# A planned TensorE order whose planner also counts the arrival of instructions, with its priorities set anew

## The chip, the core and the metric

The kernel runs on one core of a Trainium2 chip. The time is device microseconds (us) of one execution, the median over runs. The core's engines are PE (TensorE; PEld is its weight loads), DVE (VectorE), ACT (ScalarE), POOL (GpSimd) and SP (SyncE, which here only issues DMAs). Each engine executes its own instructions strictly in the order of the program; between engines there are semaphores.

## The reference

Three stages follow each other. Stage 1 is a delta-rule recurrence over 768 positions, for 2 batches of 8 heads of width 48; stage 2 a dense block over the 1536 tokens that it yields; stage 3 a mixture of 8 experts, one expert for each token.

```python
for t in range(S):                                   # stage 1
    y[:, :, t] = np.einsum('bhd,bhde->bhe', q[:, :, t], state)
    v_old = np.einsum('bhde,bhd->bhe', state, kt)    # kt: normalised k
    state = state + bt[..., None] * np.einsum('bhd,bhe->bhde', kt, vt - v_old)
h = x @ w_in                                         # stage 2: 1536x384 @ 384x1024
solu = h * softmax(h)
x = layernorm(solu) * g_ln @ w_out                   # back to 1536x384
logits = x @ w_gate; expert_idx = argmax(logits)     # stage 3
y = relu(x[of expert e] @ w1[e]) @ w2[e]             # scattered back, times the gate
```

## The kernel before, in words

**Stage 1** cuts the 768 positions into 24 chunks of 32, in 3 groups of 8 chunks (numbered 0 to 2). A group is first solved, without the recurrence: products of its keys and queries (`gram`, L522, tile G), a triangular solve on DVE (`prep`: transposition L593, 28 small steps L602 and L605, transpositions L613 and L615), and then the joins of its halves (`join`, L635 and L650, tile Z). Then `stream` walks through its chunks, one after the other, because each needs the state of the one before: the state times keys and queries (L717, tile X), DVE's subtraction (L722, R), the solved triangle times it (L730), scaling on ACT (L738) and DVE (L696), the state's increment (L745, dS), DVE's addition (L690, S), and the chunk's output (L759). The first L717 of chunk 8 thus waits for the solve of group 1, that of chunk 16 for the solve of group 2.

**Stage 2** goes by rows of 128 tokens, 12 of them; four chunks give two rows. A row's function `rows` transposes it (L884, xp), multiplies by w_in (L912, 18 matmuls of 512 columns, tile h), takes maximum, exponential and product on DVE and ACT (L922, L926, L930), transposes back (L951, lp), and multiplies by w_out (L961, 24 matmuls, tile xb). The weights come as 64-bit words and are converted once, in 6 blocks of w_in and 8 of w_out: a load (L785), four DVE operations (L793, L795, L798, L801), a split in two halves on ACT and POOL (L808, L810), and for w_out a small product with the gate weights on PE (L840, tp; L850, gp).

**Stage 3**, from the first L1398 on, has an order written out by hand, which the change does not touch.

**What sets the order.** Stages 1 and 2 are written as coroutines (chains: `rows`, `stream`, `prep`, `wi_block` and so on). When the program is built, the class `Flow` runs them through a list scheduler: each chain asks for an engine with an expected duration, and of the chains that could start, the one with the lowest priority number goes next (`_pick`). The priorities stand in the table `PR` (L54). `Flow.use` books a TensorE step; where TensorE would have nothing to do, `run` puts filler matmuls (L1250) there. The order in which the chains are served becomes the order of the instructions on PE, DVE, ACT and POOL, and of the DMAs on SP; nothing of it is decided at run time.

On SP a DMA waits only where its data or buffer does. `loads_1` (`PR['l1']`) loads group 1's inputs, and starts with a tiny gate DMA (L402, `kn<-A`) that reads a result of group 0, so that everything behind it in SP's order starts only then. `f32_block` (L785; `PR['wi']`) loads a block of w_in; its chain also waits for the planner's event `early`, but the DMA itself has no such wait: it is held back only by what stands ahead of it on SP.

An instruction of the source is not always one on the chip. An fp32 matmul of stage 1 is executed as two, each with its own weight load: "x16" in the program's order is 32 matmuls in the trace, and 64 instructions.

Of the kernel before, what the change touches and what calls it, by code (L numbers as in the profile page):

```python
# [25 lines left out]
DM = H * D  # L26
# [4 lines left out]
E = 8  # L31
# [19 lines left out]
EVA = (0, 1, 1)  # L51
HB = 0
HC = C // 2
PR = {'m0': 4.99, 'x0': 4.63, 'g1': 4.24, 'g2': 3.44, 'lg': 6.61, 'l1': 1.43, 'l2': 3.47, 'wi': 2.29, 'wo': 5.01, 'wog': 1.18, 'n1': 1.36, 'n2': 4.17, 'p1': 4.79, 'p2': 8.87, 'v': 8.16, 'y': 5.65, 'rows': 2.82, 'sx': 3.04, 'xt': 6.94, 'lt': 3.58, 'ft': 2.8}  # L54
PASSES = ((0, 0), (0, 1), (1, 0))
PE, DVE, ACT, POOL, DMA = range(5)
DENSE = 0
# [51 lines left out]
class Flow:  # L109
# [2 lines left out]

    TICK, COLS, FILL = 3.4133, 2800, (0.215, 0.43, 512, 32)
    LAT = {PE: 0.2, DVE: 0.13, ACT: 0.15, POOL: 0.08, DMA: 2.0}

    def __init__(self, pace, cap, until):
        self.req = {e: [] for e in self.LAT}
        self.free = {e: 0.0 for e in self.LAT}  # L120
        self.pending = deque()
        self.cur = None
        self.rate, self.cap, self.fill = pace * self.COLS / self.TICK, cap, None
        self.level = self.at = 0.0
        self.floor, self.until = 1500, until
        self.cols = {}
        self.banks, self.fill_bank = {}, "h"
        self.mode, self.pool = DENSE, 0.0
        self.n = self.live = 0
# [107 lines left out]

    def use(self, t, us):
        cold = not self.warm(t)
        mode = us[3] if len(us) > 3 else DENSE  # L240
        us, cols = us[cold] + (0.0 if mode == self.mode else 0.22 if cold else 0.115), us[2]
        self.mode = mode
        i, f = divmod((t + us) / self.TICK, 1)
        f = min(1, f * self.TICK / us)
        self.cols[int(i)] = self.cols.get(int(i), 0) + cols * f
        self.cols[int(i) - 1] = self.cols.get(int(i) - 1, 0) + cols * (1 - f)
        self.level = min(self.cap, max(-self.floor, self.level - self.rate * (t + us - self.at)) + cols)
        self.at = self.free[PE] = t + us
        return us


def _mm(n):

    return 0.448e-3 * n + 0.003, n / 1200 + 0.002, n

KQ, BLK, DS, GRAM2, GRAM1, WG = (0.96, 1.65, 520, 1), (0.37, 0.62, 152, 2), (0.67, 1.14, 634, 1), \  # L260
    (0.52, 0.88, 520, 3), (0.44, 0.72, 320, 3), (0.7, 1.4, 50)


def _dv(n):
# [16 lines left out]
def build(tc, I, out, cap, dbg=None, pace=1.15, room=100):  # L281
# [7 lines left out]
    pactx = ExitStack()  # L289
    fl = Flow(pace, room, PR['ft'] * 10)  # L290

    with ctx:
# [261 lines left out]
        def grams(g, cs, kss):  # L554
            for ks in kss:
                for c in cs:
                    yield from gram(g, c, ks)
                    fl.loose()
# [8 lines left out]
        def prep(g):  # L567
# [11 lines left out]
            AM[g] = (A, M, mw)  # L579
            fl.spawn(grams(g, range(0, GC, 2), ((0, 1),)), (prio, PR['g1'], PR['g2'])[g])  # L580
            if g:
# [81 lines left out]
        xt = {}  # L663
# [9 lines left out]
        def y_copy(c):  # L673
            s, j = divmod(c, 4)
            for r in range(4):
                if r:
                    fl.loose()
                yield ACT, _ac(192), False, f"X{c % 2}"
                p = 32 * (r ^ 1)
                nc.scalar.copy(out=xt[s][32 * j:32 * j + 32, :, 96 * r:96 * r + 96]  # L680
                               .rearrange("p b (l d) -> p b l d", l=2),
                               in_=ps_[c % 2][p:p + 32, :, r % 2].rearrange("p (b l) d -> p b l d", b=2))
            event("s1", c).set()
            if j == 3:
                for b in range(B):
                    tile_x(b, s)
# [13 lines left out]
        def stream():  # L700
# [3 lines left out]
            for c in range(NC):  # L704
# [51 lines left out]
                for q in range(4):  # L756
                    for r in range(4):
                        p, t = 32 * r, 32 * (r ^ 1)
                        nc.tensor.matmul(ps[t:t + 32, q, r % 2], lhsT=M[p:p + 32, cc * 4 + q],  # L759
                                         rhs=ub[p:p + 32, q, r % 2], start=False, stop=True, skip_group_check=True)  # L760
                fl.spawn(y_copy(c), PR['y'])
                if c < NC - 1:
# [4 lines left out]
        wi = [s2w.tile([128, KT, F], F32R, name=f"wi{k}") for k in range(2)]  # L767
        wo = [s2w.tile([128, FT, DM + E], F32R, name=f"wo{k}") for k in range(2)]
# [51 lines left out]
        def wo_block(t):  # L820
# [12 lines left out]
        def wo_gate(t, wf):  # L833

            yield WT_
            yield T_
            yield PE, (KT * 0.109, KT * 0.2, KT * 250)
            tp = psT.tile([128, KT, 128], F32, name="tp", tag="t")
            for k in range(KT):
                nc.tensor.transpose(tp[:, k], wf[:, 128 * k:128 * k + 128], idn)  # L840
            event("wT", t).set()
            yield ACT, _ac(DM)
            wT = wd.tile([128, KT, 128], F32, name="wT")
            nc.scalar.copy(out=wT, in_=tp)
            T_.release()
            yield T_
            yield PE, WG
            gp = psT.tile([128, E], F32, name="gp", tag="t")
            for k in range(KT):
                nc.tensor.matmul(gp, lhsT=wT[:, k], rhs=wg[:, k], start=(k == 0), stop=(k == KT - 1))  # L850
            WT_.release()
            yield DVE, _dv(E)
            nc.vector.tensor_copy(out=wo[0][:, t, DM:], in_=gp)
            yield DVE, _dv(E)
            nc.vector.tensor_tensor(out=wo[1][:, t, DM:], in0=gp, in1=wo[0][:, t, DM:].bitcast(F32), op=ALU.subtract)
            T_.release()
            event("wog", t).set()


        xbx = psH.tile([128, 512], F32, name="xb")  # L860
        nc.vector.memset(xbx[0:32, DM + E:], 0.0)
        xb = xbx[:, :DM + E]
# [6 lines left out]
        def tile_x(b, s):  # L869
            fl.spawn(rows(b, s), PR['rows'] + 0.01 * count[0])  # L870
            count[0] += 1

        def rows(b, s):
            j = b * TPB + s
            x = xt[s][:, b]
            if dbg and "x" in dbg:
                nc.sync.dma_start(out=dbg["x"][128 * j:128 * j + 128], in_=x)
            prio, fl.cur.prio = fl.cur.prio, PR['xt'] + 0.01 * j
            yield XT_
# [18 lines left out]
            h = h_.popleft()  # L898
            event("h", j).set()
            if fl.fill_bank == "h":  # L900
                fl.fill_bank, fl.FILL, spare[0] = "xb", (0.056, 0.11, 120, 32), xbx[0:32, DM + E:]
            fl.cur.prio = prio
            for n in range(2):
                for i, (a, w) in enumerate(PASSES):
# [14 lines left out]
            lg = s2.tile([128, 4, E], F32, name="lg", bufs=4)  # L919
# [50 lines left out]
            lt, m8, i8, le = (lg[:, k] for k in range(4))  # L970
# [275 lines left out]
        spare = [h_[0][0:32, :512]]  # L1246
# [136 lines left out]
        for e in range(E):  # L1383
            n = CAPS[e]
# [184 lines left out]
```

## Time and profile before

| | before |
|---|---|
| median of 3 runs | 478.85 us (477.11 to 483.55) |
| profiled execution | 477.91 us, of which its span 476.1 us |
| stages 1 and 2 (to the first L1398 matmul) | 325.0 us of the span |
| PE busy | 425.9 us (89%) |
| DVE busy | 291.8 us (61%) |
| filler matmuls (L1250) | 145 |

The span runs from the first to the last instruction. Busy shares say little by themselves: what a stage waits for is seen in its stretch. In a timeline, "[2.55 <-issue]" ahead of an instruction is idle time of the engine in which it waited for nothing that the profile shows. A row "x32" is 32 instructions, and successive PE groups overlap by a few hundredths of a microsecond. A row of the windows has the stretch, its length, each engine's busy time with the number of instructions, then PE's granted clock as a share, the DMA engines' busy share and GB/s.

### The profile page before, as it was taken

The page shows a single profiled execution, that of the slowest core. Times are in us where ns is not written, and L with a number is a line of the kernel's source. Part 1 is how long each engine was busy: PE and PEld are TensorE (multiplying, and loading weights), DVE is VectorE, ACT ScalarE, POOL GpSimd, SP SyncE. Part 2 cuts the span into 40 slices and gives each one's busy share as a digit, 9 for nine tenths or more (in the row PEclk, how much of TensorE's full clock was granted, in tenths as well). Part 3 has the DMA queues.
Part 4 walks back from the last instruction along what each step waited for, and adds up shares of the span by engine and source line. Part 5 has one row for each costly group of instructions (what it writes and reads, how often), then busy time and mean ns, then how long its engine had stood idle before and what let it go on. Part 6 is the DMA issues. An engine that isn't in the chain of part 4 may idle for free.

```text
span 476.1 us, 16248 instructions
## 1 busy us (share of the span) xinstructions
PE 425.9 (89%) x6941; PEld 374.2 (79%) x6941; DVE 291.8 (61%) x839; ACT 240.8 (51%) x556; POOL 168.8 (35%) x177
## 2 busy tenths in 40 slices
PE   2328978989999999999999999999999999999983
PEld 2228765767787887867677899898999999999982
DVE  5698998885222668845365587655566555456630
ACT  3023574866223644626354676544665666567520
POOL 1303753112031130021022233323685469658811
PEclk9999995988659999999999999999999999999998
DMA  8265342241000402202111311305984567568000
GB/s 313 84 252 183 134 158 71 66 159 65 4 3 6 168 3 87 100 12 96 69 37 36 134 35 44 140 35 167 361 267 140 189 222 251 190 215 274 17 25 29
DMA packets 17076, 57.57 MB, mean 121 GB/s; under 512 B 2456, under 2 KB 8454, under 8 KB 16226
## 3 DMA queue, kind: packets, MB, share of 16 engines
q1 hardware_dynamic: 15170, 51.70, 31.4%
q0 software_dynamic: 1824, 4.73, 2.7%
q8 instruction: 56, 0.92, 0.8%
q14 instruction: 26, 0.21, 0.1%
HBM read 45.96 MB, written 11.13 MB: 120 GB/s over the span
## 4 chain that ended last, share of the span: by engine, by line
PE 72%; DVE 13%; issue 5%; ACT 4%; DMA 3%; POOL 1%; SPq 0%; POOLq 0%; DVEq 0%; ACTq 0%
PE h L912 12%; PE u L1398 12%; PE xb L961 11%; PE o L1343 10%; PE X L717 5%; PE dS L745 3%; PE G L522 3%; PE lp L951 2%; PE X L759 2%; PE o L1436 2%; DMA out<-y,ti 2%; PE Z L650 2%; PE X L730 1%; DMA kqT<-kqT 1%; DVE wu L798 1%
## 5 line engine op out<-in xcount | busy, mean ns | idle before, releaser
L1215 POOL TENSOR_TENSOR wh<-wr,wh 128x512 fp32r<-128x512 f32 x64 | 81.3, 1301 | 22.7 <-ACT wh L1213 18.6
L912 PE MATMUL h<-wi,xT 128*128 128x512 f32 x216 | 66.6, 434 | 0.0
L961 PE MATMUL xb<-wo,lT 128*128 128x392 f32 x288 | 63.5, 360 | 0.0
L1343 PE MATMUL o<-wh,hT 128*128 128x384 f32 (+1 forms) x336 | 63.1, 340 | 0.0
L1398 PE MATMUL u<-xdT,wh 128*128 128x240 f32 (+1 forms) x504 | 60.4, 278 | 2.2 <-DVE hT L1402 2.2
L1398 PEld LDWEIGHTS u<-xdT,wh 128*128 128x128 f32 x504 | 59.0, 189 | 2.8 <-DVE hT L1402 2.6
L1343 PEld LDWEIGHTS o<-wh,hT 128*128 128x128 f32 (+1 forms) x336 | 57.5, 182 | 0.2
L961 PEld LDWEIGHTS xb<-wo,lT 128*128 128x128 f32 x288 | 50.1, 191 | 2.3
L912 PEld LDWEIGHTS h<-wi,xT 128*128 128x128 f32 x216 | 39.6, 199 | 8.2
L1213 ACT CAST wh<-wr 128x512 fp32r<-128x512 f32 x67 | 41.0, 616 | 3.4 <-DMA wr<-w 3.4
L680 ACT COPY xt<-X 32x192 f32<-32x192 f32 x96 | 29.7, 310 | 25.7 <-PE X L759 24.4
L1402 DVE SCALAR_TENSOR_TENSOR hT<-u,hT 128x240 fp32r<-128x240 f32 (+2 forms) x64 | 24.8, 408 | 26.4 <-ACT hT L1401 26.3
L1401 ACT ACTIVATE hT<-u 128x240 fp32r<-128x240 f32 (+2 forms) x64 | 23.9, 376 | 24.0 <-PE u L1398 21.3
L717 PEld LDWEIGHTS X<-S,kqT 48*64 48x64 f32 x768 | 28.2, 153 | 5.2 <-issue 3.8
L522 PE MATMUL G<-kqT 48*32 48x64 f32 x768 | 19.8, 269 | 13.1 <-DMA kqT<-kqT 8.5
L717 PE MATMUL X<-S,kqT 48*64 48x48 f32 x768 | 31.3, 238 | 0.0
L1355 POOL DMA_INDIRECT out<-y,ti x17 | 16.5, 971 | 38.9 <-DMA out<-y,ti 11.4
L522 PEld LDWEIGHTS G<-kqT 48*32 48x32 f32 x768 | 16.5, 140 | 15.6 <-DMA kqT<-kqT 8.5
L1121 POOL DMA_INDIRECT xs<-xo,posi x12 | 12.5, 1043 | 41.1 <-ACT lT L990 13.6
L738 ACT ACTIVATE ub<-X,slot 128x96 f32<-128x96 f32 x48 | 13.7, 337 | 26.1 <-PE X L730 25.1
L1209 DVE CAST wh<-wp 128x512 fp32r<-128x512 f32 x29 | 20.0, 691 | 9.8 <-ACT wp L1208 8.5
L745 PE MATMUL dS<-ub,kn 64*48 64x96 f32 x368 | 23.8, 279 | 2.2 <-ACT ub L738 2.2
(197 smaller groups left out, 763.9 us busy)
## 6 DMA issues: line engine op xcount, KB each, us to landing
wr<-w SPq DMA_DIRECT2D x32, 768.0 KB, 5.4
kqT<-kqT SPq DMA_DIRECT2D x6, 1024.0 KB, 9.0
xs<-z SPq DMA_DIRECT2D x5, 772.0 KB, 3.9
w<-w_in SPq DMA_DIRECT2D x6, 512.0 KB, 4.9
w<-w_out SPq DMA_DIRECT2D x8, 384.0 KB, 3.1
kn<-kN SPq DMA_DIRECT2D x3, 768.0 KB
vt<-vN SPq DMA_DIRECT2D x3, 768.0 KB, 6.9
xd<-xs SPq DMA_DIRECT2D x10, 193.0 KB, 4.7
```

What stands on the lines that cost most here:

```text
L522: nc.tensor.matmul(G[32 * r:32 * r + 32, c2 * 4 + Q], lhsT=kq[:, r1], rhs=x, start=True, stop=True)
L680: nc.scalar.copy(out=xt[s][32 * j:32 * j + 32, :, 96 * r:96 * r + 96] .rearrange("p b (l d) -> p b l d", l=2), in_=ps_[c % 2][p:p + 32, :, ...
L717: nc.tensor.matmul(ps[64 * o:64 * o + 64, q, r1], lhsT=T[p, c % HG, q // 2, r1, q % 2], rhs=S_[p, q, r1], start=(q == 0 and r1 == 0), stop ...
L745: nc.tensor.matmul(dS[64 * o:64 * o + D, q], lhsT=kn_t[g][64 * o:64 * o + 64, cc, q], rhs=ub[64 * o:64 * o + 64, q], start=False, stop=Tru ...
L912: nc.tensor.matmul(h[:, FH * n:FH * n + FH], lhsT=xT[a][:, k], rhs=wi[w][:, k, FH * n:FH * n + FH], start=(m == 0), stop=(m == 3 * KT - 1))
L961: nc.tensor.matmul(x2, lhsT=lT[t // 4][a][:, t % 4], rhs=wo[w][:, t], start=(t == 0 and i == 0), stop=(t == FT - 1 and i == 2))
L1213: nc.scalar.copy(out=hl[0][:, cs], in_=r[:, cs])
L1215: (nc.vector if k == 1 else nc.gpsimd).tensor_tensor(out=hl[1][:, cs], in0=r[:, cs], in1=hl[0][:, cs].bitcast(F32), op=ALU.subtract)
L1343: nc.tensor.matmul(o, lhsT=hT[t][a][:, s:s + n], rhs=w[k][:, t % 4], start=(t == 0 and i == 0), stop=(t == FT - 1 and i == 2))
L1398: nc.tensor.matmul(u, lhsT=w[c][:, k, f0:f0 + 128], rhs=xT[a][:, k], start=(i == 0 and k == 0), stop=(i == 2 and k == KT - 1))
L1401: nc.scalar.activation(out=hh[0], in_=u, func=AF.Relu)
L1402: nc.vector.scalar_tensor_tensor(out=hh[1], in0=u, scalar=0.0, in1=hh[0].bitcast(F32), op0=ALU.max, op1=ALU.subtract)
```

## The change

The planner's TensorE step gets a count of instructions. After each 256 of them, the next step cannot end before the preceding 256 were begun plus `FETCH` = 3.0 us. Each kind of step says how many instructions it has (64 for a join's half, 64 for L717, 32 for L745, 2 for a plain matmul). And 18 of the 21 priorities are different numbers. No instruction is added or taken out besides fillers: 145 before, 115 in the change. The rest is order. Lines from L126 on have 1 to 5 higher numbers in the changed kernel.

```diff
-PR = {'m0': 4.99, 'x0': 4.63, 'g1': 4.24, 'g2': 3.44, 'lg': 6.61, 'l1': 1.43, 'l2': 3.47, 'wi': 2.29, 'wo': 5.01, 'wog': 1.18, 'n1': 1.36, 'n2': 4.17, 'p1': 4.79, 'p2': 8.87, ...
+PR = {'m0': 0.85, 'x0': 5.4, 'g1': 6.06, 'g2': 3.58, 'lg': 6.61, 'l1': 2.05, 'l2': 6.4, 'wi': 1.84, 'wo': 2.59, 'wog': 1.5, 'n1': 1.36, 'n2': 6.31, 'p1': 6.27, 'p2': 9.01, ...
...
-    TICK, COLS, FILL = 3.4133, 2800, (0.215, 0.43, 512, 32)
+    TICK, COLS, FILL, FETCH = 3.4133, 2800, (0.215, 0.43, 512, 32, 2), 3.0
...
-        mode = us[3] if len(us) > 3 else DENSE
+        mode, n = us[3] if len(us) > 3 else DENSE, us[4] if len(us) > 4 else 2 * max(1, round(us[2] / 250))
         us, cols = us[cold] + (0.0 if mode == self.mode else 0.22 if cold else 0.115), us[2]
         self.mode = mode
+        self.sent += n
+        if self.sent >= 256:
+            us = max(us, self.there - t + us / 2)
+            self.sent, self.there = self.sent - 256, t + us + self.FETCH
...
-KQ, BLK, DS, GRAM2, GRAM1, WG = (0.96, 1.65, 520, 1), (0.37, 0.62, 152, 2), (0.67, 1.14, 634, 1), \
-    (0.52, 0.88, 520, 3), (0.44, 0.72, 320, 3), (0.7, 1.4, 50)
+KQ, BLK, DS, GRAM2, GRAM1, WG = (0.96, 1.65, 520, 1, 64), (0.37, 0.62, 152, 2, 64), (0.67, 1.14, 634, 1, 32), \
+    (0.52, 0.88, 520, 3, 64), (0.44, 0.72, 320, 3, 64), (0.7, 1.4, 50, DENSE, 12)
```

Since the order changes nearly everywhere, three places are shown.

**SP, start of the program.** In the kernel before, behind the loads of group 0 (the last is vt):

```order
L413 DMA wg<-w_gate 128x24
L393 DMA vt<-vN 128x1536
L402 DMA kn<-A 1x1
L785 DMA w_339<-w_in 128x1024
L375 DMA kn<-kN 128x1536
L384 DMA kqT<-kqT 128x2048 x2
L785 DMA w_505<-w_in 128x1024
```

And in the change:

```order
L418 DMA wg<-w_gate 128x24
L398 DMA vt<-vN 128x1536
L790 DMA w_335<-w_in 128x1024
L790 DMA w_341<-w_in 128x1024
L407 DMA kn<-A 1x1
L398 DMA vt<-vN 128x1536
L380 DMA kn<-kN 128x1536
```

Two loads of w_in now stand ahead of the gate DMA `kn<-A` instead of behind it.

**DVE, where the solve of group 1 begins** (the transposition `L<-A`). Before, in chunk 4 (its R is the row above), while the weight block w_1084, the 8th of 14, is converted:

```order
L801 SCALAR_TENSOR_TENSOR wu<-w_996,wu 128x384
L793 TENSOR_SCALAR wu<-wu 128x384
L795 TENSOR_SCALAR wu<-wu 128x384
L798 SCALAR_TENSOR_TENSOR wu<-w_1084,wu 128x384
L722 TENSOR_TENSOR R<-X_136,vt 128x384
L801 SCALAR_TENSOR_TENSOR wu<-w_1084,wu 128x384
L593 STREAM_TRANSPOSE L<-A 128x32x32
```

And in the change, in chunk 6, behind the 12th weight block (w_1273) and behind the maximum and the product of row 0:

```order
L927 TENSOR_REDUCE sm_1371<-h 128x1
L897 TENSOR_TENSOR xT_1428<-xp,xT_1427 128x384
L727 TENSOR_TENSOR R<-X_136,vt 128x384
L935 ISA p,sm_1371<-h,e 128x1024
L935 ISA sm_1371 128x1
L701 TENSOR_TENSOR ub<-dS,slot 128x192
L798 TENSOR_SCALAR wu<-wu 128x384
L800 TENSOR_SCALAR wu<-wu 128x384
L803 SCALAR_TENSOR_TENSOR wu<-w_1273,wu 128x384
L858 CAST wo_142<-gp 128x8
L806 SCALAR_TENSOR_TENSOR wu<-w_1273,wu 128x384
L860 TENSOR_TENSOR wo_143<-gp,wo_142 128x8
```

The next row there is L598, the transposition. It has moved back by two chunks, four weight blocks and the first half of row 0's softmax.

**PE, chunk 18**, from its L717 to that of chunk 19. Before, the joins of group 2 (Z) stand one by one between w_in matmuls (h):

```order
L717 MATMUL X_136<-S,kqT 64x48 x16
L635 MATMUL Z<-Tt,A 32x16 x16
L912 MATMUL h<-wi_140,xT_3592 128x512 x3
L730 MATMUL X_136<-R,Tt 32x48 x8
L730 MATMUL dS<-R,Tt 32x48 x8
L912 MATMUL h<-wi_141,xT_3592 128x512 x3
L745 MATMUL dS<-ub,kn 48x96 x8
L912 MATMUL h<-wi_140,xT_3593 128x512
L759 MATMUL X_136<-ub,M_2046 32x48 x16
L912 MATMUL h<-wi_140,xT_3593 128x512 x2
L717 MATMUL X_137<-S,kqT 64x48 x16
```

And in the change they stand together, with no w_in or w_out matmul in the chunk:

```order
L722 MATMUL X_136<-S,kqT 64x48 x16
L640 MATMUL Z<-Tt,A 32x16 x48
L735 MATMUL X_136<-R,Tt 32x48 x8
L735 MATMUL dS<-R,Tt 32x48 x8
L655 MATMUL Z<-z,Tn 32x16 x32
L750 MATMUL dS<-ub,kn 48x96 x8
L764 MATMUL X_136<-ub,M_2214 32x48 x16
L655 MATMUL Z<-z,Tn 32x16 x16
L722 MATMUL X_137<-S,kqT 64x48 x16
```

The chunk has 96 join products instead of 16, and none of its nine long matmuls, which now stand ahead of chunk 16.

## Rows read from the trace of the kernel before

**Rows 1.** The page: granted clock in 40 slices; the DMA queue of instructions.
```profile
PEclk9999995988659999999999999999999999999998
q8 instruction: 56, 0.92, 0.8%
```
**Rows 2.** Windows of two stretches: chunks 8 to 10, and the tail.
```profile
120.00:144.00 24.00, 22.97 (x648) 19.78 (x647) 5.45 (x13) 6.78 (x22) 4.41 (x7) 0.57 0.01 3
268.00:325.00 57.00, 55.98 (x380) 50.49 (x379) 38.47 (x164) 31.92 (x66) 19.15 (x25) 1.00 0.23 82
```
**Rows 3.** Timeline of PE, 8 to 19 us: start, length, what, idle before.
```profile
8.54 3.64 PE L522 MATMUL G<-kqT 48*32 48x64 f32 x128 [8.54 <-DMA kqT<-kqT]
13.96 3.64 PE L522 MATMUL G<-kqT 48*32 48x64 f32 x128 [1.78 <-issue]
```
**Rows 4.** Timeline of PE around 70 us and around 129 us.
```profile
69.32 0.63 PE L522 MATMUL G<-kqT 48*32 48x64 f32 x26
72.50 0.43 PE L522 MATMUL G<-kqT 48*32 48x64 f32 x6 [2.55 <-issue]
...
127.02 0.42 PE L635 MATMUL Z<-Tt,A 32*32 32x16 f32 x26
127.37 1.13 PE L717 MATMUL X<-S,kqT 48*64 48x48 f32 x32
128.43 0.73 PE L650 MATMUL Z<-z,Tn 32*32 32x16 f32 x64
129.16 0.28 PE L730 MATMUL X<-R,Tt 32*32 32x48 f32 x6
130.47 0.44 PE L730 MATMUL X<-R,Tt 32*32 32x48 f32 x9 [1.03 <-issue]
```
**Rows 5.** Windows around the first stalls, and of a later load of w_in.
```profile
10.00:12.00 2.00, 2.00 (x84) 1.94 (x75) 0.92 (x4) 0.02 (x1) 0.84 (x1) 1.00 0.85 333
12.00:14.00 2.00, 0.22 (x12) 0.07 (x7) 0.90 (x3) 0.00 (x0) 1.91 (x3) 1.00 0.02 6
...
70.00:72.00 2.00, 0.00 (x0) 0.00 (x0) 1.90 (x7) 1.39 (x3) 0.00 (x0) 1.00 0.17 27
...
45.00:47.00 2.00, 2.00 (x56) 1.91 (x58) 1.97 (x2) 0.92 (x3) 2.00 (x2) 1.00 0.91 291
```
**Rows 6.** Timeline of SP's DMA issues, 0 to 24 us.
```profile
18.10 0.73 SPq L402 DMA_DIRECT2D kn<-A  x1
18.89 0.34 SPq L785 DMA_DIRECT2D w<-w_in  x1
```
**Rows 7.** DVE: window from the solve's start to its end; its last transposition (timeline).
```profile
74.20:99.00 24.80, 22.23 (x356) 16.68 (x348) 22.65 (x66) 17.09 (x40) 3.83 (x4) 0.83 0.17 50
97.80 1.17 DVE L615 STREAM_TRANSPOSE Tn<-L 128x512 f32<-128x512 f32 x1
```
**Rows 8.** DVE's groups, 68 to 100 us, shapes apart: busy, mean ns.
```profile
L801 DVE SCALAR_TENSOR_TENSOR wu<-w,wu 128x384 int32<-128x384 int32 x5 | 3.2, 643 | 0.0
L798 DVE SCALAR_TENSOR_TENSOR wu<-w,wu 128x384 int32<-128x384 int32 x5 | 2.8, 550 | 0.0
...
L795 DVE TENSOR_SCALAR wu<-wu 128x384 int32<-128x384 int32 x5 | 1.8, 351 | 0.0
...
L922 DVE TENSOR_REDUCE sm<-h 128x1 f32<-128x1024 f32 x1 | 1.2, 1224 | 0.0
```
**Rows 9.** Timeline of PE: chunk 8 begins; prices of steps.
```profile
120.13 1.95 PE L717 MATMUL X<-S,kqT 48*64 48x48 f32 x32
...
88.37 0.73 PE L850 MATMUL gp<-wg,wT 128*128 128x8 f32 x6
...
284.37 4.53 PE L961 MATMUL xb<-wo,lT 128*128 128x392 f32 x24
291.32 2.33 PE L912 MATMUL h<-wi,xT 128*128 128x512 f32 x9
298.63 1.54 PE L1250 MATMUL x0p<-ones 128*32 128x120 bf16 x26
```

More of the change, by code (lines that the diff above doesn't have):

```diff
@@ L53 @@
 HC = C // 2
-PR = {'m0': 4.99, 'x0': 4.63, 'g1': 4.24, 'g2': 3.44, 'lg': 6.61, 'l1': 1.43, 'l2': 3.47, 'wi': 2.29, 'wo': 5.01, 'wog': 1.18, 'n1': 1.36, 'n2': 4.17, 'p1': 4.79, 'p2': 8.87, 'v': 8.16, 'y': 5.65, 'rows': 2.82, 'sx': 3.04, 'xt': 6.94, 'lt': 3.58, 'ft': 2.8}
+PR = {'m0': 0.85, 'x0': 5.4, 'g1': 6.06, 'g2': 3.58, 'lg': 6.61, 'l1': 2.05, 'l2': 6.4, 'wi': 1.84, 'wo': 2.59, 'wog': 1.5, 'n1': 1.36, 'n2': 6.31, 'p1': 6.27, 'p2': 9.01, 'v': 8.16, 'y': 8.79, 'rows': 4.66, 'sx': 6.48, 'xt': 0.95, 'lt': 6.9, 'ft': 3.96}
 PASSES = ((0, 0), (0, 1), (1, 0))
@@ L125, in __init__ @@
         self.floor, self.until = 1500, until
+        self.sent, self.there = 0, 0.0
         self.cols = {}
@@ L252, in _mm @@
 def _mm(n):
-    return 0.448e-3 * n + 0.003, n / 1200 + 0.002, n
-KQ, BLK, DS, GRAM2, GRAM1, WG = (0.96, 1.65, 520, 1), (0.37, 0.62, 152, 2), (0.67, 1.14, 634, 1), \
-    (0.52, 0.88, 520, 3), (0.44, 0.72, 320, 3), (0.7, 1.4, 50)
+    return 0.448e-3 * n + 0.003, n / 1200 + 0.002, n, DENSE, 2
+KQ, BLK, DS, GRAM2, GRAM1, WG = (0.96, 1.65, 520, 1, 64), (0.37, 0.62, 152, 2, 64), (0.67, 1.14, 634, 1, 32), \
+    (0.52, 0.88, 520, 3, 64), (0.44, 0.72, 320, 3, 64), (0.7, 1.4, 50, DENSE, 12)
 def _dv(n):
@@ L900, in rows @@
             if fl.fill_bank == "h":
-                fl.fill_bank, fl.FILL, spare[0] = "xb", (0.056, 0.11, 120, 32), xbx[0:32, DM + E:]
+                fl.fill_bank, fl.FILL, spare[0] = "xb", (0.056, 0.11, 120, 32, 2), xbx[0:32, DM + E:]
             fl.cur.prio = prio
```

## Prediction

> **What bounds the kernel now.** The page's slices come first: PE's granted clock dips below nine tenths only in slices 7 and 9 to 12 of 40, between 71 and 143 us [rows 1]. So the windows by stage are next. The tail from 268 us has 55.98 of 57.00 us of PE at full clock; the stretch from 120 to 144 us is as full (22.97 of 24.00), but at a mean granted clock of 0.57, mostly the lower of the two levels (1.2 GHz) [rows 2]. There PE is busy and slow: the 32 matmuls of L717 take 1.95 us at 120.13 and 1.13 us at 127.37, where the clock was up [rows 4, 9]. From about 144 us on the time is the sum of PE's work; what an order can change there is fillers and small waits. Before 120 us it is a chain over all engines, with DVE at 22.65 of 24.80 us while it solves group 1 [rows 7].
>
> The third view is PE's timeline, for waits put down to "issue". The reader is to count matmuls between them. After 128 matmuls of G the next starts 1.78 us late [rows 3]. From 127.02 to the stall behind 129.16 there are 26 + 32 + 64 + 6 = 128 again, then 1.03 us of nothing [rows 4]. 128 matmuls with their weight loads are 256 instructions, and the page's queue of instructions moved 0.92 MB in 56 packets, 16.4 KB or 256 instructions of 64 bytes each [rows 1]. So instructions arrive in blocks of 256, and where PE uses a block up too fast, it stands. From 127.02 to 130.47 a block took 3.45 us, with DMA share 0.01 there [rows 2, 4]. That is what the planner's FETCH = 3.0 means to count.
>
> How late a block comes depends on the DMAs. The stall that ends at 13.96 follows DMA at a share of 0.85 until 12 us, and 0.02 behind it [rows 3, 5]; the longest, 2.55 us to 72.50, has its block arrive only when the share has fallen to 0.17 [rows 4, 5]. Both look as if the block stood behind data that were queued earlier.
>
> **The change, part by part.** The sum is for chunk 8's start, then for what is left behind it. Chunk 8 is the place to cut, since the order ahead of it is a chain and behind it a sum of PE's work. It begins at 120.13 [rows 9].
>
> *Two loads of w_in go ahead of the gate.* Before, they were issued at 18.89 and later, behind the gate at 18.10 [rows 6]. Now nothing holds them, and they join the queue behind group 0's inputs, at about 4 us. They are 512 KB each, 1.05 MB; at 333 GB/s, the rate of that queue [rows 5], 3.1 us, at the 291 GB/s of a later w_in load [rows 5] 3.6 us. The second block of instructions, which ended the 1.78 us stall, would come that much later, and all behind it: two more products, their masks, the solve. Nothing covers it, since that stall is on the chain already. I take +3.0; bounds 0 (the block overtakes the data) and +3.6.
>
> *The solve of group 1 moves back on DVE.* In the program's order, the DVE operations ahead of the end of its last transposition (L615) are more by: four weight blocks save two L793s and single L795 and L798, 4 x 0.64 + 3 x 0.55 + 3 x 0.35 + 2 x 0.35 = 6.0 us [rows 8]; and one chunk's three operations (1.4), a row's maximum [rows 8] and its product (1.2 each), one xT (0.5), two lT (1.4), eight reads of gp and six statistics of a row (0.16 each, 2.3), together 8.0 (the maximum has its row here; the others are estimates between it and the 0.35 of L795). 14.0 us more work at DVE's share there, 22.65 / 24.80 = 0.91 [rows 7], is 15.3 us. In addition chunk 6's state addition now stands behind the transposition and five solve steps, and so chunk 7 waits: I estimate 1.5. L615 ended at 97.80 + 1.17 = 98.97 [rows 7]; now at 98.97 + 15.3 + 1.5 = 115.8. Bounds: 14.0 at full share, or 16.5 and 3 if DVE waits more.
>
> *From there to chunk 8.* Before, 21 us lay between, because joins stood between gp, tp and w_out work. Now the order has, from the first join: 32 + 32 + 64 + 64 + 32 join matmuls, at 0.73 per 64 [rows 4] 2.6 us, three of w_out and nine of w_in, 0.5 and 2.1 (4.53 / 24 and 2.33 / 9, less overlap [rows 9]), and the eviction and scaling of the first join, an estimated 1.2. The joins may start 1.2 us ahead of 115.8, when L613 is done: 115.8 - 1.2 + 6.4 = 121.0. With the loads 124.0: **+3.9 against 120.1**. Bounds: 118.2 and 127.3.
>
> *Work done by then.* Chunk 8's place in PE's order has 54 w_in matmuls ahead of it instead of 36, 24 of w_out instead of 18, two more weight transpositions and one more of a row, two more gp groups, and 32 joins fewer: 18 x 0.236 + 6 x 0.182 + 3 x 0.42 + 2 x 0.66 - 0.4 = 4.2 + 1.1 + 1.3 + 1.3 - 0.4 (rows less the 0.07 to 0.2 by which they overlap [rows 4, 9]; the 0.42 for a group of three transpositions is an estimate from gp's six matmuls). **-7.5**: it is no longer to be done after chunk 8, where PE is the sum.
>
> *Fillers.* All but one of the 145 stood behind chunk 8; of the 115 now 19 stand ahead of it, in the wait for the solve. 144 - 96 = 48 x 0.0575 (1.54 for 26 [rows 9]): **-2.8**.
>
> *Losses behind chunk 8.* Two that go against each other. The run of short matmuls behind the joins, in which the clock fell, is two chunks long instead of three: w_out matmuls come in at chunk 10. Most of 24 us at 0.57 cost 1.95 instead of 1.13, about 10 us [rows 2, 4, 9]; I give back 2.6. But the joins of group 2 now stand together. From L717 of chunk 18 to that of chunk 19 there are 32 + 96 + 32 + 64 + 16 + 32 + 32 = 304 matmuls, 2.4 blocks; at 3.45 a block [rows 4] 8.2 us, where the work itself is about 5 and an ordinary chunk loses 0.7. That and the run ahead of chunk 16 (1.75 blocks, 6.0 us for about 4.8) cost 2.5 + 1.2 = 3.7. Before, the long h matmuls stood between and covered it. **+1.1**; bounds -3 (no run of slow clock) and +6 (all of it, and group 2's solve late by 2).
>
> Sum: 3.9 - 7.5 - 2.8 + 1.1 = -5.3. Against the profiled execution, 477.9 - 5.3 = 472.6; the median of the runs, 478.85, is 0.9 above that execution, so I say **473**. Stage 3 is the same instructions.
>
> **Rivals.**
> - *The block overtakes the loads*, as turns between queues would have it. For: only two stalls bear on it. Against: both end as the data do [rows 5]. 473 - 3 = 470. The Trainium skill (DMA: Bandwidth & Descriptors, section Queues, rings and completion order) has such a rule: each DMA engine takes turns between the queues that have work, packet by packet. No row here shows a block that passed.
> - *There is no such wait*, blocks come ahead of need, and the planner counts what is not there. Then the +3.0 and the 3.7 for the joins fall away: 466. Against: three waits, two of them behind exactly 128 matmuls [rows 3, 4]. This is how the Trainium skill has it (Runtime: NRT & Kernel Launch, section Instruction fetch mechanics): blocks of 256 instructions, with the crossing into the next "mostly hidden". The trace agrees on the 256 and not on the hiding.
> - *The gain comes in full*: DVE reaches the transposition without more waits, the blocks pass the data, and the w_in and w_out work now ahead of chunk 8 keeps the clock up through the joins. For: before chunk 8 PE gets 7.5 us more of long matmuls. Chunk 8 at 119, losses -3: -1.1 - 7.5 - 2.8 - 3 = -14.4 at the most; I put it at 466.
> - *Slower: the second solve starves PE.* PE serves in order, and its first join of group 1 stands behind everything that was put ahead of it. If DVE ends the solve late, PE has nothing else, and each us is lost. The mechanism is DVE standing in front of L593 for the mask of A, which on POOL now stands behind four weight subtractions. For: DVE can pass nothing that stands ahead of its next instruction. Against: the weights concerned are converted some 8 us of DVE work earlier. The point: slower than before once the solve ends 5.3 us after 118.8 (with the loads), over 2% slower 15 us after it, at 134. With 16 us: 484.
> - *The gain is eaten*: slow clock through chunk 11 and full price of the runs, +5: 478, no change.
>
> **Chances.** The forecast 0.50 (its own range 468.5 to 477), the block overtaking 0.12, no such wait 0.03, the full gain 0.15, starvation 0.08, the gain eaten 0.12. About 2% (9.6 us) is what a measurement of this kernel tells from no change; the lower bound, 469.3, is met by the full gain, by the case without waits and by a third of the overtaking: faster 0.22, slower 0.08, the same 0.70. The range from 465 to 481 leaves out most of the starvation and the end of the full gain.
>
> **What would show it.** First term: the second G group starts at 17 instead of 13.96. Second: L593 of group 1 near 95, L615 ending near 119. Third: chunk 8 at 124. Fourth: L717 of chunk 18 to 19 takes 8 us with "issue" inside. Fifth: u (stage 3) starts near 320 instead of 325. I am wrong where PE waits for more than the plan knows: then a wait of PE on DVE at L635 is among the longest in the list, or where chunk 8 is early and still nothing is gained.

## The result, and the profile of the changed kernel

The changed kernel takes 484.52 us (median of 13 runs, 481.56 to 488.2) where the kernel before took 478.76 beside it (13 runs, 476.11 to 483.55). The ratio is 1.0122, 95% interval 1.0098 to 1.0146: slower by 1.2%, where 473 us and a gain of 5.3 us were forecast. On another chip, in the last series of experiments, it was 1.0088 (1.0054 to 1.0121). The profiled execution took 482.12 us (477.9 before), its span is 480.3 us (476.1 before), so 4.2 us are to be explained.

Two lines of the page (TensorE's granted clock in 40 slices; the chain that ended last, by engine):

```profile
PEclk9655665979969999999788999999999999999998
PE 73%; DVE 12%; issue 7%; DMA 3%; ACT 3%; POOL 0%; SPq 0%; POOLq 0%; DVEq 0%; ACTq 0%
```

"issue" had 5% of that chain on the page of before and has 7% now: of a span of 480 us, some 10 us more. The clock's slices mislead in the first fifth. They read 6, 5, 5 where [rows 1] read 9, but the record of the clock in the trace of before has no entry ahead of 62 us, and L717 of chunk 0 (L722 in the changed kernel; its lines are 5 higher there) took the same in both. Timeline of PE, before:

```profile
36.71 1.95 PE L717 MATMUL X<-S,kqT 48*64 48x48 f32 x32
```

and changed:

```profile
39.05 1.95 PE L722 MATMUL X<-S,kqT 48*64 48x48 f32 x32
```

1.95 us is the price at the lower level [rows 9]; both kernels ran their first chunks there. So the prediction's reading that the clock dips only between 71 and 143 us [rows 1] does not hold, and the granted clock of 1.00 in the first window of before, below, is not measured.

The account that tells where the time went is PE's busy and idle time between four marks: the first join, chunk 4, chunk 8 (where L717 of the chunk begins) and the first u of stage 3. Windows between the marks; columns: stretch, length, then busy time of PE, of its weight loads, DVE, ACT and POOL, PE's mean granted clock, DMA share, GB/s. Before:

```profile
31.39:68.26 36.87, 31.74 (x1185) 28.15 (x1185) 33.74 (x58) 18.50 (x49) 19.68 (x17) 1.00 0.42 139
68.26:120.13 51.87, 44.87 (x865) 34.95 (x859) 40.67 (x111) 33.63 (x77) 11.49 (x14) 0.83 0.28 95
120.13:324.93 204.80, 200.97 (x3606) 165.06 (x3605) 117.78 (x427) 99.20 (x237) 41.87 (x60) 0.95 0.17 59
```

Changed:

```profile
30.85:76.64 45.79, 33.47 (x1161) 29.36 (x1161) 37.75 (x68) 22.49 (x59) 21.85 (x19) 0.57 0.37 119
76.64:129.95 53.31, 51.22 (x914) 41.31 (x914) 39.60 (x117) 32.77 (x76) 9.49 (x13) 0.87 0.27 90
129.95:328.28 198.33, 189.70 (x3552) 157.12 (x3543) 114.70 (x412) 97.12 (x231) 41.71 (x59) 0.94 0.17 60
```

Idle is length less busy. Differences of the changed kernel, beside what the prediction's terms come to in the same marks:

| stretch | busy, idle before | busy, idle changed | difference | forecast |
|---|---|---|---|---|
| up to the first join | 31.39 in all | 30.85 in all | -0.5 | +3.0 (first term) |
| first join to chunk 4 | 31.74, 5.13 | 33.47, 12.32 | busy +1.7, idle **+7.2** | with the next line: |
| chunk 4 to chunk 8 | 44.87, 7.00 | 51.22, 2.09 | busy +6.4, idle -4.9 | busy +7.5, idle -6.6 |
| chunk 8 to the first u | 200.97, 3.83 | 189.70, 8.63 | busy -11.3, idle **+4.8** | busy -10.3, +1.1 |
| first u to the end | 151.2 in all | 152.0 in all | +0.8 | 0 |

(Forecast between the first join and chunk 8: chunk 8 later by 3.9, of which 3.0 came ahead of the first join, so 0.9 longer with 7.5 more work in it.) The work moved as forecast, and the waits between chunks 4 and 8 were filled as forecast. What was not seen are 7.2 us of new idle time ahead of chunk 4 and 4.8 instead of 1.1 behind chunk 8.

The idle time ahead of chunk 4 is mostly "issue". Timeline of PE, before:

```profile
36.06 0.71 PE L650 MATMUL Z<-z,Tn 32*32 32x16 f32 x35 [1.11 <-issue]
40.34 0.23 PE L635 MATMUL Z<-Tt,A 32*32 32x16 f32 x2 [0.72 <-issue]
```

and changed:

```profile
34.15 0.71 PE L640 MATMUL Z<-Tt,A 32*32 32x16 f32 x34 [1.83 <-issue]
37.98 0.66 PE L655 MATMUL Z<-z,Tn 32*32 32x16 f32 x34 [1.73 <-issue]
41.98 0.66 PE L640 MATMUL Z<-Tt,A 32*32 32x16 f32 x34 [0.45 <-issue]
48.18 0.29 PE L655 MATMUL Z<-z,Tn 32*32 32x16 f32 x3 [4.08 <-issue]
62.12 0.37 PE L735 MATMUL X<-R,Tt 32*32 32x48 f32 x16 [1.79 <-DVE R L727]
67.72 1.94 PE L722 MATMUL X<-S,kqT 48*64 48x48 f32 x32 [1.37 <-DVE S L695]
```

The first four stand 255, 256 and 256 recorded instructions of PE apart (matmuls and weight loads), so each waits for a block of instructions. With a fifth of 0.35 at 60.03, PE waited 8.4 us for blocks in this stretch, where before it waited 1.8: that is 6.6 of the 7.2 us. Its other waits, for DVE and ACT, came to 3.8 us against 3.3. The fourth row, 4.08 us in the last joins of group 0, is longer than any of before (2.55 [rows 4]). What was in the queues then, by the same kernel's windows of 2 us:

```profile
42.00:44.00 2.00, 2.00 (x128) 1.99 (x128) 0.71 (x3) 1.46 (x5) 0.14 (x1) 0.50 1.03 324
44.00:46.00 2.00, 0.10 (x7) 0.00 (x0) 0.81 (x4) 0.66 (x1) 0.00 (x0) 0.50 0.86 352
46.00:48.00 2.00, 0.00 (x0) 0.00 (x0) 0.00 (x0) 0.00 (x0) 0.00 (x0) 0.50 0.05 20
```

and who put it there, by its timeline of SP (start, length, what was issued):

```profile
20.54 0.43 SPq L389 DMA_DIRECT2D kqT<-kqT  x1
34.72 5.81 SPq L790 DMA_DIRECT2D w<-w_in  x2
40.57 0.43 SPq L389 DMA_DIRECT2D kqT<-kqT  x1
```

Before, both k/q tiles of group 1 (1 MB each) went out together at 20.16. Now the second stands behind two blocks of w_in, and SP waits with these for buffers that DVE has to free. So 512 KB and 1 MB start at 40.2 and 40.57, in the middle of the joins. The block that follows the one entered at 41.98 arrives only when those data are nearly through. That the data hold it up is so far a reading; the next three experiments test it.

### The profile page after: what moved, and what is told of

Its sections match the earlier page's. It is cut to its first block, busy times and chain, and to the rows that moved or that the text cites. A ratio compares the mean times of both kernels' runs of the same rounds, so it can differ in the third digit from the quotient of the medians.

```text
span 480.3 us, 16189 instructions
## 1 busy us (share of the span) xinstructions
PE 422.0 (88%) x6911; PEld 372.8 (78%) x6911; DVE 291.2 (61%) x839; ACT 240.7 (50%) x556; POOL 168.9 (35%) x177
## 4 chain that ended last, share of the span: by engine, by line
PE 73%; DVE 12%; issue 7%; DMA 3%; ACT 3%; POOL 0%; SPq 0%; POOLq 0%; DVEq 0%; ACTq 0%
PE h L917 11%; PE u L1403 11%; PE xb L966 11%; PE o L1348 10%; PE X L722 5%; PE dS L750 4%; PE G L527 3%; PE lp L956 2%; PE X L764 2%; DMA out<-y,ti 2%; PE Z L640 2%; PE o L1441 2%; PE Z L655 2%; DMA kqT<-kqT 2%; DVE wu L806 1%
## 5 line engine op out<-in xcount | busy, mean ns | idle before, releaser
L966 PE MATMUL xb<-wo,lT 128*128 128x392 f32 x288 | 65.6, 364 | 0.0
L722 PEld LDWEIGHTS X<-S,kqT 48*64 48x64 f32 x768 | 29.0, 157 | 7.3 <-issue 5.0
L722 PE MATMUL X<-S,kqT 48*64 48x48 f32 x768 | 32.3, 242 | 2.5 <-DVE S L695 1.4
L727 DVE TENSOR_TENSOR R<-X,vt 128x384 f32<-128x384 f32 x24 | 13.3, 556 | 26.6 <-PE X L722 26.0
L527 PE MATMUL G<-kqT 48*32 48x64 f32 x768 | 18.8, 255 | 12.0 <-DMA kqT<-kqT 8.9
L527 PEld LDWEIGHTS G<-kqT 48*32 48x32 f32 x768 | 15.2, 131 | 15.3 <-DMA kqT<-kqT 8.9
L640 PE MATMUL Z<-Tt,A 32*32 32x16 f32 x768 | 12.2, 194 | 15.6 <-DVE Tt L618 12.8
```

The lines of the kernel that those rows point to most:

```text
L527: nc.tensor.matmul(G[32 * r:32 * r + 32, c2 * 4 + Q], lhsT=kq[:, r1], rhs=x, start=True, stop=True)
L722: nc.tensor.matmul(ps[64 * o:64 * o + 64, q, r1], lhsT=T[p, c % HG, q // 2, r1, q % 2], rhs=S_[p, q, r1], start=(q == 0 and r1 == 0), stop ...
L966: nc.tensor.matmul(x2, lhsT=lT[t // 4][a][:, t % 4], rhs=wo[w][:, t], start=(t == 0 and i == 0), stop=(t == FT - 1 and i == 2))
```

## The experiments

A ratio is to the kernel before, on the same chip, with its 95% interval.

### The k/q tile sent early

Only SP's order differs from the changed kernel; the planner's own times, and with them the order of PE, DVE, ACT and POOL, stay.

```diff
-kqT[t] = raw.tile(..., name="kqT", bufs=4)
+for i in {2: (2, 3), 3: ()}.get(t, (t,)): kqT[i] = raw.tile(..., name="kqT", bufs=4)
...
-nc.sync.dma_start(out=kqT[t]..., in_=I["kqT"][:, HG * t:HG * t + HG])
+for i in {2: (2, 3), 3: ()}.get(t, (t,)): nc.sync.dma_start(
+    out=kqT[i]..., in_=I["kqT"][:, HG * i:HG * i + HG])
```

> The changed kernel with one thing moved, on SP alone: the load of the second k/q tile of group 1 is issued right behind the first one, ahead of the third and fourth w_in block, instead of behind them (it went out at 40.57). Order on all compute engines as in the changed kernel. Theory 1 (a load that is queued late holds up the next block of TensorE's instructions): the stall of 4.08 us in the join at 44.09 shrinks to 0.5 to 1.8 as the other stalls of that stretch, chunk 1 starts near 48 instead of 50.96, and 2 to 4 us of it reach the end: 480.5 to 482.5 against 484.5. Rival (the order on VectorE bounds chunks 2 to 8, so that an early stall is made good by chunk 8): the stall goes, chunk 8 stays at 129 to 130 and the time at 484 to 485. Second rival (the block is late whatever is loaded, since 256 instructions were used up within 3.4 us): the stall stays at 3 us or more.

Measured 1.0017 (0.9985 to 1.0048); the range given is 1.004 to 1.008 as a ratio, so the gain is a little larger than forecast. Timeline of SP:

```profile
20.09 1.18 SPq L389 DMA_DIRECT2D kqT<-kqT  x2
34.31 14.04 SPq L790 DMA_DIRECT2D w<-w_in  x3
```

and of PE, the same kernel:

```profile
40.35 0.66 PE L640 MATMUL Z<-Tt,A 32*32 32x16 f32 x34 [1.55 <-issue]
43.81 0.28 PE L655 MATMUL Z<-z,Tn 32*32 32x16 f32 x3 [1.34 <-issue]
```

The 4.08 us became 1.34, chunk 1 starts at 46.59 instead of 50.96, and the gain is not lost again on the way: chunk 8 starts at 124.13 instead of 129.95. The rival that DVE bounds chunks 2 to 8 falls; so does the one that the block is that late whatever is loaded.

### The same tile sent still later

```diff
+if t != 3:  # in load_kq: tile 3 is not issued here
     nc.sync.dma_start(out=kqT[t]..., ...)
...
 nc.sync.dma_start(out=r..., in_=src...); w_n.append(m)   # a block of w_in
+if len(w_n) == 5: nc.sync.dma_start(out=kqT[3]..., in_=I["kqT"][:, HG * 3:HG * 4])
```

> The changed kernel with the load of the second k/q tile of group 1 put one w_in load further back on SP, so that it goes out near 52 instead of 40.57; TensorE's order is that of the changed kernel. Theory (the harm is that the load's data stand ahead of the instruction block that is asked for at 42, not that the load comes late for its reader): the stall of 4.08 us in the join shrinks to 1.0 to 2.0 as when it went out early, and the time falls by 2 to 5 us, unless the tile is then late for its own reader at 65 (landing near 58). Rival (an early load is what helps: something reads the tile, or a buffer hangs on it): stall as in the changed kernel, 484 to 486 where before gives 479.

Measured 1.0047 (1.0028 to 1.0066), 2.0 to 3.6 us under the changed kernel by its two ratios. Timeline of SP:

```profile
48.69 0.43 SPq L791 DMA_DIRECT2D kqT<-kqT  x1
```

and of PE, the same kernel:

```profile
44.10 0.28 PE L655 MATMUL Z<-z,Tn 32*32 32x16 f32 x3 [1.62 <-issue]
```

Sent later than in the changed kernel (48.69, not near 52), the tile does not hurt that block either: 1.62 us. So the harm was the collision, not lateness. (Over the profiles of the changed kernel and its edits, that stall was 4.1 to 4.9 us in the four with the tile where the change puts it, and 1.3 to 1.9 us in the five with the tile moved.)

### The tile sent late in the kernel before

The same edit in the kernel before, there behind the third block of w_in (`len(w_n) == 3`).

> The kernel before with one thing moved, on SP alone: the load of the second k/q tile of group 1 goes behind the second and third w_in load (out near 36.6 instead of 20.6). Theory (data queued ahead of an instruction block hold it up wherever the order of the engines comes from): a block between 36 and 44 comes 1 to 3 us later than the 0.72 us stall of before, chunk 1 starts 1.5 to 3 us later than 44.80, and the time rises by 1.5 to 4 us (ratio 1.003 to 1.008). Rival (the stall belongs to the changed order of joins): ratio 0.998 to 1.002.

Measured 1.0026 (1.0005 to 1.0047). Timeline of SP:

```profile
36.51 0.44 SPq L786 DMA_DIRECT2D kqT<-kqT  x1
36.99 0.43 SPq L393 DMA_DIRECT2D vt<-vN  x1
```

and of PE, the same kernel:

```profile
40.01 0.23 PE L635 MATMUL Z<-Tt,A 32*32 32x16 f32 x2 [0.45 <-issue]
46.08 0.45 PE L759 MATMUL X<-ub,M 32*32 32x48 f32 x10 [2.38 <-issue]
52.55 0.29 PE L730 MATMUL X<-R,Tt 32*32 32x48 f32 x2 [2.48 <-issue]
```

The block stall goes where the data go: 2.38 us behind 43.7, where before had none, and chunk 1 starts at 46.93 instead of 44.80, as forecast. The block after it waits 2.48 us more, also with loads in the queue (v of group 1 and the next kn went out at 36.99 and 43.75). The delay is not made good in stages 1 and 2. Chunk 4 starts at 71.77 instead of 68.26, chunk 8 at 123.75 instead of 120.13, the first u at 328.54 instead of 324.93, each 3.5 to 3.6 us later. Between chunks 4 and 8 the idle time is 7.00 us as it was:

```profile
71.77:123.75 51.98, 44.98 (x867) 35.13 (x860) 40.67 (x111) 33.68 (x77) 11.49 (x14) 0.83 0.28 96
```

The profiled executions differ by 2.5 us, the ratio over all runs gives 1.2 us, just under the range. Why the whole shows less than stages 1 and 2 of the profile stays open.

### The joins of group 2 spread

```diff
-fl.spawn(join(g, c, A, Tt), prio + 0.01 * c)
+fl.spawn(join(g, c, A, Tt), ((4.0, 4.0, 9.01, 9.01)[c // 2] if g == 2 else prio) + 0.01 * c)
```

> The changed kernel with the joins of group 2 spread among h and xb matmuls (priority of its first two joins 4.0 in place of 9.01), the order up to chunk 16 the same but for the last 20 us before it. Theory 2 (bare runs of joins behind chunk 15 lose time twice, by the instruction blocks and by the slow clock that follows: stalls of 1.12 and 1.42, slow stretches 227.5 to 234.3 and 247.9 to 254.8): neither slow stretch is there, no stall over 0.5 us between 210 and 260, and the time falls by 4 to 7 us, to 478 to 480. Rival (the time behind chunk 15 is set by the sum of TensorE's work and the joins cost the same wherever they stand): within 1 us of 484.5.

Measured 1.0010 (0.9985 to 1.0035). Against the changed kernel's 1.0122, taken on another chip, that is a gain of 5.4 us, within the 4 to 7 forecast (on one chip, below, it is 3.2). The size came out, the reason given for it did not. What it was to remove, timeline of PE of the changed kernel:

```profile
226.66 1.32 PE L722 MATMUL X<-S,kqT 48*64 48x48 f32 x32 [1.12 <-issue]
...
246.76 0.86 PE L750 MATMUL dS<-ub,kn 64*48 64x96 f32 x15 [1.42 <-issue]
```

Those are gone; the one that remains there is 0.84 us at 241.27, and the lower clock is granted in one stretch (242.5 to 252.7) instead of two. But from chunk 8 to the first u the spread kernel took 200.81 us, where the changed kernel took 198.33: no gain where the waits were taken away. Theory 2 does not hold as put, and that the size fits it is luck; see the repeat.

### The two halves of the change

> The planner that counts the instruction blocks, with the priorities of before. Loads on SP in the order of before. Theory (the loss comes from the new priorities: the loads ahead of the gate, the solve of group 1 behind other work on VectorE, the bare joins of group 2): 476 to 480, same as before. Rival (the count itself puts work in a worse order, since it assumes 3.0 us for a block where it takes 3.4 to 3.8): 482 or more.

Measured 1.0257 (1.0202 to 1.0312): some 12 us slower than before and 6 us slower than the changed kernel. The theory is refuted; the rival's time is met, but its reason, the 3.0 us, was not tested.

> The planner of before with the new priorities. The load of the second k/q tile of group 1 stands behind two w_in loads as in the changed kernel. Theory (the priorities carry the loss): 484 to 488, with an instruction stall of over 3 us between 40 and 50. Rival (the priorities are sound and the count spoils them): 474 to 479.

Measured 1.0197 (1.0154 to 1.0239), 490 us, slower than theory and rival had it. It has the forecast stall, 4.81 us at 42.66.

Waits for instruction blocks between the first join and the first u (idle over 0.25 us in front of the instruction at which a block of 256 begins, added up from the trace): before 5.4 us, count alone 5.6, priorities alone 12.3, changed 13.5 (14.0 on the other chip). The count, which was to make the plan avoid these waits, leaves them where they are with either set of priorities; the new priorities more than double them. Each half alone is slower than both together, for reasons beyond the blocks. With the count alone, PE's other waits of this length grew from 9.1 to 17.2 us, the record has the lower clock for 54.6 us instead of 37.5, and there are 213 fillers. With the priorities alone chunk 8 came early, at 119.37, but from there to the first u it took 219.8 us (198.3 in the changed kernel), with 153 fillers. That the priorities suit the planner that they were chosen with is a guess that fits both; it was not tested.

### Both edits, and all of it on one chip

> The two edits of the first two experiments together: the second k/q tile of group 1 sent ahead of two w_in loads, and the joins of group 2 spread. Theory (two separate losses, 1.05% and 1.1% of the changed kernel, one ended by chunk 2 and one begun behind chunk 15): they add, 474 where before gives 479 (ratio 0.990, within 0.987 to 0.994); instruction stalls between the first join and the first u sum to 7 us or less, against 13.45 in the changed kernel. Rival (both give back the same slack, since VectorE or the loads bound the middle): no better than either alone, ratio 1.000 to 1.002.

Measured 0.9979 (0.9958 to 0.9999): lower than either, and short of the sum; "issue" waits over 0.25 us came to 8.9 us, not 7 or less. As the ratios came from several chips, four kernels were run again on one:

> The changed kernel itself, on the chip on which the three below run, since its ratio of 1.0122 was taken on another. Both theories: 1.009 to 1.015.

> The k/q tile sent early, again. Theory that the two edits' gains overlap (together they gave 0.9979 where 0.990 was expected): 1.000 to 1.004 beside a changed kernel at 1.012. Rival (the chip of the first run flattered it): 1.005 to 1.008, and the gains add.

> The joins of group 2 spread, again. Theory that the gains overlap: 1.000 to 1.003. Rival (they add, and this one was flattered): 1.004 to 1.008.

> Both edits, again. 0.996 to 1.000 by either; where it stands against the product of the two above, each over the changed kernel, says whether the gains add (0.990 if the first measurements of each were right).

| kernel | ratio | interval | median us (before 480.00) |
|---|---|---|---|
| changed | 1.0088 | 1.0054 to 1.0121 | 483.99 |
| k/q tile early | 1.0036 | 1.0008 to 1.0063 | 480.91 |
| joins spread | 1.0021 | 0.9992 to 1.0050 | 481.54 |
| both | 0.9976 | 0.9955 to 0.9997 | 478.89 |

The tile gives 0.5%, the joins 0.7%, both 1.1%. If the gains add, both edits should give 1.0036 x 1.0021 / 1.0088 = 0.9969; 0.9976 was measured, so here they add within the intervals. Each edit alone fell into the range of the theory that they overlap, but that range counted from a changed kernel at 1.012, which on this chip stands at 1.0088. The shortfall of the first measurement of both is accounted for in the same way: it set ratios of different chips against each other. With both edits the plan is at or just ahead of the kernel before.

Where the tile's gain lies is seen in the windows. Repeat of the changed kernel, from the first join to chunk 4, to chunk 8, to the first u:

```profile
30.31:75.52 45.21, 34.60 (x1162) 30.59 (x1162) 37.24 (x68) 22.53 (x59) 21.93 (x19) 0.84 0.38 119
75.52:127.79 52.27, 50.18 (x915) 40.57 (x914) 39.56 (x116) 32.78 (x76) 9.45 (x13) 0.88 0.27 93
127.79:328.55 200.76, 191.05 (x3552) 157.94 (x3544) 114.76 (x412) 97.12 (x231) 41.64 (x59) 0.93 0.17 60
```

With the tile early:

```profile
30.47:72.21 41.74, 33.09 (x1162) 29.30 (x1162) 36.93 (x67) 22.23 (x58) 21.65 (x19) 0.96 0.33 103
72.21:125.46 53.25, 51.16 (x914) 41.24 (x913) 39.86 (x117) 33.00 (x77) 9.80 (x13) 0.87 0.27 92
125.46:326.16 200.70, 191.30 (x3553) 158.49 (x3544) 114.82 (x412) 97.10 (x231) 41.60 (x59) 0.93 0.17 60
```

Chunk 4 comes 3.3 us earlier. The stretch ahead of it is 3.5 us shorter: 2.0 in idle time (10.61 to 8.65) and 1.5 in busy time, at a granted clock of 0.96 instead of 0.84 in the record; whether the tile brought that too was not tested. From chunk 4 on it takes 0.9 us longer, so the first u comes 2.4 us earlier.

Joins spread, from the first join to chunk 8 and to the first u:

```profile
30.69:127.77 97.08, 85.31 (x2075) 71.54 (x2075) 76.81 (x183) 55.22 (x134) 31.41 (x31) 0.86 0.32 105
127.77:327.66 199.89, 191.17 (x3573) 155.47 (x3564) 116.02 (x414) 97.14 (x231) 42.15 (x59) 0.96 0.17 61
```

Five profiles have the joins of group 2 together (the changed kernel, its repeat, and the three with the tile moved alone), four have them spread. Chunk 8 to the first u took 200.4 us on average with the joins together and 200.1 spread: against the waits and the slow clock that were taken away stand 21 more fillers and a slow stretch at another place. The gain stands behind the first u: 153.6 us on average with the joins together, 151.5 spread. Half of that is one wait in the last expert. Timeline of PE in the changed kernel:

```profile
458.63 5.31 PE L1403 MATMUL u<-xdT,wh 128*128 128x240 f32 x45 [1.70 <-DVE hT L1407]
```

in its repeat:

```profile
459.15 6.93 PE L1403 MATMUL u<-xdT,wh 128*128 128x240 f32 x45 [2.12 <-DVE hT L1407]
```

and with both edits, repeated:

```profile
455.49 5.31 PE L1403 MATMUL u<-xdT,wh 128*128 128x240 f32 x45 [0.29 <-DVE hT L1407]
```

The wait was 1.7 to 2.4 us in the five with the joins together and 0.3 to 1.6 in the four with them spread; before had 1.57. The other half is the clock that follows. In three of the five, the repeat (460.4 to 463.8) among them, the lower clock was granted for 3.4 us from some 1.2 us behind this wait on, and the same 45 matmuls took 6.9 us instead of 5.3. The two others and all four with the joins spread had no such stretch. Stage 3 has the same instructions in all of them. Why the order in stage 2 shows there was not tested and stays open.

## Why the prediction was wrong

The step that failed is in the second term: it took the stretch from the first join to chunk 4 over unchanged from before, and 7.2 us of new idle time arose there, 6.6 of it in waits for blocks of instructions. The first term failed too, to the other side: it put such a wait where there was none.

**The first term (+3.0 ahead of the first join) was a misreading.** The 1.78 us in front of the second G group [rows 3] are no wait for a block. The program has two buffers for G (`psT`, bufs=2), and PE may write the first again only when DVE's two operations on it, the second into M, have read it. Timeline of DVE, before:

```profile
13.44 0.41 DVE L540 TENSOR_TENSOR M<-G,mup 128x256 f32<-128x256 f32 x1
```

This second read ends at 13.85 and G goes on at 13.96 [rows 3]. In the kernel with the k/q tile early, where the two loads of w_in are ahead of the gate as in the changed kernel, the read ends 0.01 us earlier and G begins 0.02 us earlier. Its timeline of DVE:

```profile
13.43 0.41 DVE L545 TENSOR_TENSOR M<-G,mup 128x256 f32<-128x256 f32 x1
```

and of PE:

```profile
13.94 3.64 PE L527 MATMUL G<-kqT 48*32 48x64 f32 x128 [2.41 <-issue]
```

The page's "issue" is time for which it shows no releaser, and 128 matmuls before it were a coincidence: two buffers of 64. The early loads did delay a block: its packets in the queue of instructions start at 14.37 in the changed kernel, 13.15 with the k/q tile early, 11.97 before. In the changed kernel's profile that shows inside the second group (16.84, after 1.49); its first part ran faster there, so the group ends only 0.5 us later, at 18.06 instead of 17.59. In the other kernels with these loads it ran through in 3.64. The first join even started earlier, at 30.85 instead of 31.39, so the term is -0.5, not +3.0: in the solve of group 0 two reductions of group 1's keys (L476, 0.55 us each) no longer stand ahead of the transposition L613, and from L593 to L613 it took 10.0 us instead of 11.0. Timeline of PE, changed kernel:

```profile
13.81 1.54 PE L527 MATMUL G<-kqT 48*32 48x64 f32 x94 [1.25 <-issue]
16.84 1.22 PE L527 MATMUL G<-kqT 48*32 48x64 f32 x34 [1.49 <-issue]
```

**The second term (chunk 8 at 124.0) failed in what it left out.** Chunk 8 started at 129.95. The solve did move back, and further than forecast (L593 and L615 are L598 and L620 here; timeline of DVE):

```profile
97.29 1.23 DVE L935 CUSTOM_DVE_ANT_0 p<-h,e 128x1024 f32<-128x1024 f32 x1 [1.77 <-ACT e L931]
...
100.63 2.15 DVE L598 STREAM_TRANSPOSE L<-A 128x1024 f32<-128x1024 f32 x1
...
124.01 1.07 DVE L620 STREAM_TRANSPOSE Tn<-L 128x512 f32<-128x512 f32 x1
```

It began at 100.63 instead of near 95, behind a row's product that waited for ACT, and ended at 125.08 instead of 119. But that is not what set chunk 8. PE has 2.09 us of idle time between chunk 4 and chunk 8, none of it in front of the joins: it was occupied with the w_in and w_out work and 19 fillers until the solve was done. What set chunk 8 was the stretch ahead of chunk 4, which the prediction took over unchanged from before. It followed two loads of w_in past the gate and did not follow the third and fourth, on SP, past the k/q tile. The tile's part is 2 to 3 us of the 7.2 (idle ahead of chunk 4 is 10.61 and 8.65 without and with the early tile on one chip, 12.32 and 9.21 by the first profiles; the stall there 4.08 and 1.34). Nearly all the rest is waits for blocks as well, with or without the tile: the joins of group 0 stand closer together in the changed order. The block entered at 41.98 was used up in 2.1 us, the one entered at 40.34 before in 3.6, and behind that one PE did not wait. With the tile early PE still waited 4.4 to 4.5 us there in three waits, against 1.8 in two before. What the closer joins cost by themselves was not tested.

**The third and fourth terms held.** 7.5 us of work were to go ahead of chunk 8 and 48 fillers to go: busy time is +8.1 ahead of chunk 8 and -11.3 behind it, forecast +7.5 and -10.3.

**The fifth term (+1.1) had the right mechanism at the wrong size.** The stretch from chunk 18 to 19 took 6.45 us (241.96 to 248.41) with 1.42 us of issue in it, not 8. But stalls behind chunk 8 came also where none were put, in the joins of group 1 (0.63, 1.44 and 0.40 us between 131.8 and 140.3), and idle time is +4.8. The 2.6 us that were given back for a shorter slow run came: the lower clock lasted 10.2 us there (135.3 to 145.5) instead of 20.3, but it was granted again at 227.5 to 234.3 and 247.9 to 254.8, behind the two runs of joins.

**The rivals.** The block overtaking the loads has the three runs of the k/q tile against it: the stall was 4.08 us with 1 MB in the queue ahead of it and 1.34 or 1.62 without, and moving the load moved the stall. The rule cited for it, that a DMA engine takes turns between its queues packet by packet (the Trainium skill, DMA: Bandwidth & Descriptors, section Queues, rings and completion order), taken alone would have let 16 KB pass early; the trace shows the block's packets only from 45.77 on, 3.8 us after the block before it was entered, and the measurement decides. The rival without waits falls: 5.4 us before, 13.5 in the changed kernel. That the crossing is "mostly hidden" (the Trainium skill, Runtime: NRT & Kernel Launch, section Instruction fetch mechanics) agrees with the trace in the h and xb work, where no such wait is seen, and not in the joins: PE used a block up in 2.1 us there (41.98 to 44.10) and stood. Starvation by the second solve did not come: the solve ended 6 us later than forecast, and PE had other work until then. (Its time is mis-added, too: 16 us on 473 are 489, not 484.) The rival that the gain is eaten was nearest and stopped at 478; no rival had a load of the later ones in the way of a block, and so the range ended below the result.

Summed by stretch, what came less what was forecast: up to the first join -0.5 - 3.0 = -3.5; to chunk 8 10.4 - 0.9 = +9.5; to the first u -6.5 + 9.2 = +2.7; stage 3 +0.8. That is +9.5 on a forecast of -5.3, the +4.2 between the two profiled executions.

## What to carry to other kernels

Where a change moves loads, list every load between its old and its new neighbours on the issuing engine, and ask of each what TensorE is doing when it will now go out: a run of short matmuls here used a block of 256 instructions up in 2.1 us and got the next some 3.5 to 4 us behind the last, and a megabyte queued in front of one cost some 3 us more, of which, in either kernel, 2.4 to 3.6 us were still missing at the first u. Put such loads ahead of the run or behind it. A wait named "issue" is not yet a wait for instructions: first look whether another engine let go of a buffer a tenth of a microsecond before it ended, and whether the break comes at the same place in every 256 instructions. And work that is moved ahead of a chain fills only the waits that lie behind the point where it becomes available; draw up busy and idle time between marks before counting on it.

## What the runs showed of the hardware

The next block of instructions came behind data that were queued when PE entered the block ahead of it. In the changed kernel PE entered one at 41.98, the packets of the next start at 45.77, when the 1.5 MB are nearly through (their last packet starts at 46.71), and PE goes on at 48.18. With the tile early the same two times are 40.35 and 41.40. In the kernel before they are 40.34 and 41.39, and 40.01 and 43.63 with its tile sent late (it landed at 43.30). Without such a load short matmuls still waited 1.3 to 1.6 us at these crossings (the rows of the tile experiments), some 3.5 to 4 us from one block to the next, where the planner assumed 3.0. At each of the two runs of joins of group 2, in which PE stood 1.1 to 2.4 us, the lower clock set in, from 1.1 us before PE went on to 1.9 us after, and lasted 6.8 to 10.3 us, in all five profiles named above that have the joins together.
